# Three crossbar transposes a unit on the SP queue, and five exponential buffers for seven, in a fused attention and gated MLP kernel

## The chip, the cores and the metric

The kernel runs on one core of a Trainium2 chip. The metric is the device time of one execution in microseconds; lower is better. A core has five engines that run their own instruction streams in order and meet through semaphores: TensorE (PE, with its weight loads shown apart as PEld), VectorE (DVE), ScalarE (ACT), GpSimd (POOL) and SyncE (SP), which here only issues DMA transfers. The transfers themselves run on 16 DMA engines.

## The reference

Attention over 4 batches and 8 heads, 576 positions, head dimension 64, with a bias that a small MLP of the relative position gives, and behind it a gated MLP on the 2304 x 512 result. All of it is float32.

```
scores = scale * q @ k.T                      # (4, 8, 576, 576)
x      = log1p(|i - j|) / log1p(max(i, 1))
scores = scores + relu(x * w1 + b1) @ w2      # a bias per head, the same for all batches
attn   = softmax(scores)
y      = (attn @ v), heads side by side       # (2304, 512)
out    = (sigmoid(y @ w_gate) * (y @ w_val)) @ w_out
```

## The kernel before, in words

There are three phases. The first builds the bias of all heads (up to about 105 us). The second is the attention, in 16 units of work; a unit is one batch and one pair of heads. The third is the gated MLP. The change lies in the attention.

A unit has nine steps, s = 0 to 8. Steps 0 to 7 each take 128 query rows of one head (four steps per head); step 8 takes the last 64 rows of both heads. Every step n of the 144 runs through one body, written out by hand (the scheduler does not reorder: `tc.manual_schedule`), so the order of the Python calls is the order of instructions on each engine:

- `score(n)`: TensorE multiplies q by k into a PSUM tile `sc` (L569). It hands back `soft`, which is called later in the same step: one VectorE instruction (L573) adds the bias, writes the negated scores to a tile `en` and gives the row minimum `mn`; one ScalarE instruction (L576) takes the exponential in place and sums the row.
- `turn(n - 2)`: two steps later TensorE transposes that `en`, four blocks of 128 x 128 (L592), into a PSUM tile `pt`, of which there are three in a ring. Out of `pt` ScalarE writes the high part `aH` (L491) and VectorE the low part `aL` (L492), each in a format TensorE takes. In steps s = 1, 4, 7 of the set `AR` ScalarE copies `pt` to SBUF (L605) and GpSimd makes both parts.
- The last 64 columns of `en` are not transposed then. In `turn` of s = 3 and s = 7, that is in step 5 and in step 0 of the next unit, four narrow transposes (L612) read the columns 512 to 576 of four `en` tiles at once: those of s - 3, s - 2, s - 1 and s. So an `en` of s = 0 is still read in step 5, and one of s = 4 in step 0 of the next unit.
- `products`: TensorE multiplies the transposed parts by v into `acc` (L654), 36 instructions a unit, `FILL[s]` of them at the end of each step; VectorE copies `acc` out as `xe` (L657) and SP stores it.

The order on VectorE inside a step: in steps of the set `SOFT` (2, 7, 5, 3) `soft` comes first and the low parts of the step before (`after`) follow it; in the other steps they come ahead of `soft`.

SP gets, over a unit: in step 0 the load of k (`kr`), in step 1 that of v (`vr`), in step 2 two small stores of row sums (`rs`), in step 3 the four copies that spread q over the tile `QS` of the next unit and the load of q (`qr`), and two stores of `xe`. Each transfer on SP is issued when its own semaphore waits are met, in order; one that waits holds up those behind it. From step 2 of unit 12 on, `extra(n)` also gives the MLP's first loads (`xin`, `xrec`, `ww`) to SP, after what the step itself issues, by a list called `PLAN`.

Tiles of SBUF come from pools. A pool `enp` with `ENB` buffers holds the `en` tiles; a new `en` takes the buffer of the one `ENB` steps back, and its first writer (L573) waits until that one's last reader is done.

Of the kernel before, what the change touches and what calls it, by code (L numbers as in the profile page):

```python
# [13 lines left out]
F16 = mybir.dt.float16  # L14
# [9 lines left out]
HF = S // 2  # L24
NCH = S // 64
FILL = (7, 0, 9, 0, 6, 3, 2, 7, 2)
ENB = 7
WM = 6
LAG, WSTEP, V0STEP, V1STEP = 2, 2, 7, 1
KSTEP, QSTEP = (4, 8), 1  # L30
# [48 lines left out]
AR = (1, 4, 7)  # L79
# [357 lines left out]
def attention(tc, att, q, k, v, biases, biasL, ident, xs, rs, extra):  # L437
# [3 lines left out]
    nc = tc.nc  # L441
    PSUM = bass.MemoryType.PSUM
    pool = lambda n, b, **kw: att.enter_context(tc.tile_pool(name=n, bufs=b, reuse_waits="tile", **kw))
# [18 lines left out]
    def load_k(u):  # L462

        p, b = units[u]
        qkraw[u, "kr"] = t = raw.tile([128, 2, S], F32, name="kr")
        for g in range(2):
            nc.sync.dma_start(out=t[64 * g:64 * g + 64], in_=k[b, 2 * p:2 * p + 2].rearrange("h d s -> d h s"))
# [22 lines left out]
    def split(hi, lo, ps):  # L490
        nc.scalar.activation(out=hi, in_=ps, func=AF.Copy)  # L491
        return lambda: nc.vector.tensor_tensor(out=lo, in0=ps, in1=hi.bitcast(F32), op=ALU.subtract)  # L492

    def pool_split(hi, lo, src):
        copy(hi, src)
        nc.gpsimd.tensor_tensor(out=lo, in0=src, in1=hi.bitcast(F32), op=ALU.subtract)  # L496

    def prep_k(u, h):
        if h == 0:
            prepped[u] = two.tile([128, 2, 2, S], F32R, name="k"), QS[u % 2]  # L500
        pool_split(prepped[u][0][:, h, 0], prepped[u][0][:, h, 1], qkraw[u, "kr"][:, h])
# [26 lines left out]
    vp = pool("vp", 1)  # L528
    enp = pool("enp", ENB)
    st = pool("st", 4)  # L530
# [2 lines left out]
    at4 = pool("at4", 2)  # L533
    ar_p = pool("arp", 2)
    xep = pool("xep", 2)
    ps_t = pool("ps_t", 3, space=PSUM)
    ps_v = pool("ps_v", 1, space=PSUM)
    ps_s = pool("ps_s", 2, space=PSUM)
# [5 lines left out]
        vsplit[u, h] = vv  # L544

    state = {}

    def score(n):
        u, s = divmod(n, 9)
        p, b = units[u]  # L550
        ks, qs = prepped[u]
        if s == 0:
            state[u] = (st.tile([128, 9], F32, name="sm"), [], [], at4.tile([128, 2, S], F32R, name="a4"), {})
        ps = ps_s.tile([128, 2, 512], F32, name="sc")
        en = enp.tile([128, S], F32, name="en")
        sm = state[u][0][:, s:s + 1]
        state[u][4][s] = en
        if s < 8:
            h, it = divmod(s, 4)
            nbias = biases[0][:, 8 * p + s] if p < 3 else biases[1][:, s]  # L560
            i = slice(128 * it, 128 * it + 128)
            w = qs[:, (S + 128) * h:(S + 128) * h + 512][:, i]
            mms = [(w, ks[:, h, 0]), (w, ks[:, h, 1])]
        else:
            nbias = biasL[:, p]
            mms = [(qs[:, 512 + 64 * h:640 + 64 * h], ks[:, h, r]) for r in range(2) for h in range(2)]
        for i, (l, r) in enumerate(mms):
            for e in range(2):
                nc.tensor.matmul(out=ps[:, e, 0:HF], lhsT=l, rhs=r[:, HF * e:HF * e + HF], start=(i == 0), stop=(i == len(mms) - 1))  # L569
        mn = st.tile([128, 1], F32, name="mn")  # L570

        def soft():
            nc.vector.tensor_tensor_reduce(  # L573
                out=half(en), in0=ps[:, :, 0:HF], in1=half(nbias), scale=-0.125, scalar=3.0e38,
                op0=ALU.add, op1=ALU.min, accum_out=mn)
            nc.scalar.activation(out=en, in_=en, func=AF.Exp, bias=mn, scale=-1.0, accum_out=sm)  # L576

        return soft

    def turn(n):  # L580

        u, s = divmod(n, 9)
        p, b = units[u]
        sm, aH, aL, a4, ens = state[u]
        en = ens[s]
        after = []
        if s in (0, 4):
            aH.append(atp.tile([128, 4, S], F32R, name="aH"))
            aL.append(atp.tile([128, 4, S], F32R, name="aL"))
        pt = ps_t.tile([128, 4, 128], F32, name="pt")  # L590
        for J in range(4):
            nc.tensor.transpose(pt[:, J], en[:, 128 * J:128 * J + 128], ident)  # L592
        if s == 8:
            for h in range(2):
                after.append(split(aH[h][:, :, 512:576], aL[h][:, :, 512:576], pt[:, :, 64 * h:64 * h + 64]))
            pt = ps_t.tile([128, 4, 128], F32, name="pt")
            nc.tensor.transpose(pt[0:64, 0], en[:, 512:576], ident)
            last = normal(u, pt)
            after.append(split(a4[0:64, :, 512:576], a4[64:128, :, 512:576], pt[0:64, 0].rearrange("p (h i) -> p h i", h=2)))
            return after + [last]  # L600
        h, it = divmod(s, 4)
        i = slice(128 * it, 128 * it + 128)
        if s in AR:
            ar = ar_p.tile([128, 4, 128], F32, name="ar")
            nc.scalar.activation(out=ar, in_=pt, func=AF.Copy)  # L605
            pool_split(aH[h][:, :, i], aL[h][:, :, i], ar)
        else:
            after.append(split(aH[h][:, :, i], aL[h][:, :, i], pt))
        if it == 3:
            pt = ps_t.tile([128, 4, 128], F32, name="pt")  # L610
            for e in range(4):
                nc.tensor.transpose(pt[0:64, e], ens[s - 3 + e][:, 512:576], ident)  # L612
            after.append(split(a4[0:64, h, 0:512], a4[64:128, h, 0:512], pt[0:64].rearrange("p e i -> p (e i)")))
        return after

    def normal(u, pt):
        p, b = units[u]
        nc.tensor.transpose(pt[0:9, 2], state[u][0], ident)
        rt = rtp.tile([9, 128], F32, name="rt")

        def leave():
            nc.vector.tensor_copy(out=rt, in_=pt[0:9, 2])
            to = rs[2 * p:2 * p + 2, S * b:S * b + S]
            nc.sync.dma_start(out=to[:, 0:512].rearrange("h (i p) -> h i p", p=128), in_=rt[0:8])
            nc.sync.dma_start(out=to[:, 512:576].rearrange("(o h) p -> o h p", o=1), in_=rt[8:9].rearrange("o (h p) -> o h p", h=2))

        return leave

    def invert(u):
        sm = state[u][0]  # L630
        nc.scalar.activation(out=sm, in_=sm, func=AF.Identity, bias=tiny)
        return lambda: nc.vector.reciprocal(out=sm, in_=sm)
# [31 lines left out]
    NU = len(units)  # L664
    with tc.manual_schedule():
        work = iter(())
        after, due, loads, slow = [], [], [], []
        for n in range(9 * NU + LAG + 1):
            u, s = divmod(n, 9)
            soft = score(n) if n < 9 * NU else None  # L670
            inverse = invert(u - 1) if s == 0 and u > 0 else None
            later = turn(n - LAG) if LAG <= n < 9 * NU + LAG else []
            if s in KSTEP and u + 1 < NU:
                prep_k(u + 1, KSTEP.index(s))
                if s == KSTEP[1] and u + 2 < NU:
                    loads.append(lambda z=u + 2: load_k(z))
            if s == QSTEP and u + 1 < NU:
                o, lower = prep_q(u + 1)
                later.append(lower)
                slow = [lambda o=o, z=u + 1: spread_q(z, o)]  # L680
                slow += [lambda z=u + 2: load_q(z)] if u + 2 < NU else []
            elif slow:
                loads, slow = loads + slow, []
            if soft and s in SOFT:
                soft()
                soft = None
            for f in after:
                f()
            for f in due:
                f()  # L690
            due, loads = loads, []
            if soft:
                soft()
            after = later
            if inverse:
                inverse()
            if s == WSTEP and 0 < u < NU:
                work = products(u - 1)
            if n == 9 * NU + LAG - 1:
                work = products(u - 1)  # L700
            for _ in range(FILL[s] if n < 9 * NU else 9):
                f = next(work, None)
                if f:
                    after.insert(0, f)
            if s == V0STEP and u < NU:
                split_v(u, 0)
            if s == V1STEP and 0 < u < NU:
                split_v(u - 1, 1)
                load_v(u)
            if n == 9 * NU:  # L710
                split_v(u - 1, 1)
            extra(n)
        for f in after:
            f()
        for f in work:
            if f:
                f()
# [562 lines left out]
```

## Time and profile before

| | us |
|---|---|
| median of 3 runs | 791.5 |
| lowest and highest | 790.57, 792.73 |
| span of the profiled execution, first to last instruction | 789.5 |
| TensorE busy | 755.9 (96%) |
| VectorE busy | 650.9 (82%) |
| ScalarE busy | 573.4 (73%) |
| GpSimd busy | 371.9 (47%) |
| DMA moved | 114.00 MB |

The profiled execution's own time is its span of 789.5 us and what a launch puts around it; the median of the runs is 2.0 us above that span. The busy times are sums over three unlike phases, so they do not say what limits the attention; the rows below are from that phase.

### The profile page before, as it was taken

Reading aid. Unit: us, or ns where it says so; the run is one execution under the profiler, and the core shown is the slowest. Engines: PE = TensorE matmul, PEld = TensorE weight load, DVE = VectorE, ACT = ScalarE, POOL = GpSimd, SP = SyncE. Lnnn points to the kernel's source line nnn. Section 1 sums busy time; section 2 is a strip of 40 time slices with the busy share of each in tenths; the row PEclk is TensorE's granted clock in tenths of the full one; section 3 lists DMA queues with packets and bytes.
Section 4 is the critical chain, followed back from the end, with each engine's and each line's share of the span. In section 5 each row is a group of like instructions: output and inputs, shape, how many; then the busy total and the mean of one; then the engine's idle time right before and its main releaser. Section 6 shows DMA issues by size and latency. Waiting matters only on the chain.

```text
span 789.5 us, 17579 instructions
## 1 busy us (share of the span) xinstructions
PE 755.9 (96%) x6358; PEld 605.0 (77%) x6358; DVE 650.9 (82%) x1329; ACT 573.4 (73%) x1222; POOL 371.9 (47%) x433
## 2 busy tenths in 40 slices
PE   7999989999999999898999999998999999999997
PEld 4888879999999998897899999964555555555553
DVE  6788888998999999997598988869998886777762
ACT  5888859989998998776676666676666667666653
POOL 2233559999999997972010120047633331534100
PEclk9999999999999999999999999999999999999999
DMA  6544444664665568735898953347612212422102
GB/s 201 157 147 128 122 109 109 182 171 137 165 173 152 146 171 220 205 122 182 302 288 240 271 151 119 124 125 195 180 56 80 81 54 76 154 65 81 54 2 80
DMA packets 66775, 114.00 MB, mean 144 GB/s; under 512 B 7808, under 2 KB 29440, under 8 KB 66688
## 3 DMA queue, kind: packets, MB, share of 16 engines
q1 hardware_dynamic: 62208, 106.78, 44.5%
q0 software_dynamic: 2560, 3.15, 2.6%
q10 hardware_dynamic: 1920, 2.95, 1.1%
q8 instruction: 50, 0.82, 0.4%
q14 instruction: 37, 0.30, 0.1%
HBM read 79.75 MB, written 23.67 MB: 131 GB/s over the span
## 4 chain that ended last, share of the span: by engine, by line
PE 73%; DVE 13%; ACT 5%; issue 3%; DMA 2%; SPq 1%; POOL 1%; ACTq 0%; DVEq 0%
PE po L928 15%; PE pg L1081 10%; PE sc L569 8%; PE acc L654 8%; PE pu L1081 7%; PE pt L592 6%; PE pu L904 6%; PE pg L904 6%; PE bps L362 3%; DVE btmp L370 2%; PE y L338 2%; ACT ind L343 1%; PE pt L612 1%; DVE bias L378 1%; DVE wv L1050 1%
## 5 line engine op out<-in xcount | busy, mean ns | idle before, releaser
L1081 PEld LDWEIGHTS <-wv 128*128 128x128 f16 x1008 | 98.1, 98 | 84.9 <-issue 9.9
L576 ACT ACTIVATE en<-en,mn 128x576 f32<-128x576 f32 x144 | 111.6, 775 | 31.1 <-DVE mn L573 29.9
L1039 POOL TENSOR_TENSOR ws<-wm 128x256 f32<-128x256 f32 x44 | 41.4, 942 | 157.6 <-DMA wm<-scratch 100.6
L569 PE MATMUL sc<-k,QS 128*128 128x288 f32 x640 | 112.1, 301 | 2.1 <-DMA QS<-part 0.8
L1081 PE MATMUL pg<-xq,wv 128*128 128x384 f16 x576 | 109.3, 326 | 3.1 <-ACT c L1107 2.3
L573 DVE CUSTOM_DVE_ANT_0 en<-sc,bias 128x576 f32<-128x576 f32 x128 | 93.8, 751 | 7.3 <-PE sc L569 6.3
L569 PEld LDWEIGHTS sc<-k,QS 128*128 128x128 f32 x640 | 92.1, 189 | 3.4 <-issue 1.0
L592 PE MATMUL pt<-ident,en 128*128 128x128 f32 x576 | 87.4, 274 | 3.6 <-DVE aL L492 2.0
L928 PE MATMUL po<-wo,gh 128*128 128x512 f16 x288 | 85.7, 379 | 0.0
L1081 PE MATMUL pu<-xq,wv 128*128 128x384 f16 x432 | 82.0, 326 | 2.2 <-DVE c L1087 2.2
L654 PE MATMUL acc<-aH,vv 128*128 128x288 f32 x240 | 76.2, 334 | 2.7 <-DVE xe L657 2.7
L980 POOL DMA_DIRECT2D xt<-xs x32 | 26.9, 1076 | 108.3 <-DMA xt<-xs 94.9
L1087 DVE TENSOR_TENSOR c<-pu,c 128x384 f32<-128x384 f32 x72 | 39.9, 555 | 41.6 <-PE pu L1081 28.1
L592 PEld LDWEIGHTS pt<-ident,en 128*128 128x128 f32 x576 | 69.0, 141 | 6.8 <-ACT en L576 2.9
L492 DVE TENSOR_TENSOR aL<-pt,aH 128x512 fp32r<-128x512 f32 (+1 forms) x112 | 66.6, 607 | 7.1 <-ACT aH L491 7.1
L362 PE MATMUL bps<-cfs,ind 128*128 128x64 bf16 x1458 | 67.4, 193 | 2.9 <-DVE bias L378 2.4
L343 ACT ACTIVATE ind<-y 128x576 bf16<-128x576 f32 x100 | 62.2, 653 | 10.0 <-PE y L338 7.7
L654 PE MATMUL acc<-aL,vv 128*128 128x288 f32 x240 | 66.9, 296 | 0.0
L362 PEld LDWEIGHTS <-ind 128*128 128x128 bf16 x1458 | 58.6, 98 | 9.2 <-DVE bias L378 4.2
L1099 ACT ACTIVATE gh<-c 128x384 f16<-128x384 f32 x48 | 25.1, 523 | 55.5 <-DVE c L1097 54.0
L496 POOL TENSOR_TENSOR aL<-ar,aH 128x512 fp32r<-128x512 f32 x48 | 62.5, 1302 | 3.9
L491 ACT ACTIVATE aH<-pt 128x512 fp32r<-128x512 f32 (+1 forms) x112 | 57.6, 529 | 1.2 <-PE pt L592 1.2
(173 smaller groups left out, 1948.2 us busy)
## 6 DMA issues: line engine op xcount, KB each, us to landing
wm<-scratch SPq DMA_DIRECT2D x48, 256.0 KB
kr<-in_k_dram SPq DMA_DIRECT2D x32, 288.0 KB
QS<-part SPq DMA_DIRECT2D x64, 144.0 KB
xs<-xe SPq DMA_DIRECT2D x32, 288.0 KB
scratch<-wm SPq DMA_DIRECT2D x27, 256.0 KB
wo<-scratch SPq DMA_DIRECT2D x24, 256.0 KB
vr<-in_v_dram SPq DMA_DIRECT2D x16, 320.0 KB
qr<-in_q_dram SPq DMA_DIRECT2D x16, 288.0 KB
```

Of the source, the lines that this page charges most:

```text
L343: nc.scalar.activation(out=o, in_=y[:, :, 0:HF], func=AF.Sigmoid, scale=float(2.0 ** 64))
L362: nc.tensor.matmul(out=o, lhsT=st, rhs=cfs[:, part], start=(part == 0), stop=(part == 2))
L492: return lambda: nc.vector.tensor_tensor(out=lo, in0=ps, in1=hi.bitcast(F32), op=ALU.subtract)
L496: nc.gpsimd.tensor_tensor(out=lo, in0=src, in1=hi.bitcast(F32), op=ALU.subtract)
L569: nc.tensor.matmul(out=ps[:, e, 0:HF], lhsT=l, rhs=r[:, HF * e:HF * e + HF], start=(i == 0), stop=(i == len(mms) - 1))
L573: nc.vector.tensor_tensor_reduce(out=half(en), in0=ps[:, :, 0:HF], in1=half(nbias), scale=-0.125, scalar=3.0e38, op0=ALU.add, op1=ALU.min, ...
L576: nc.scalar.activation(out=en, in_=en, func=AF.Exp, bias=mn, scale=-1.0, accum_out=sm)
L592: nc.tensor.transpose(pt[:, J], en[:, 128 * J:128 * J + 128], ident)
L654: nc.tensor.matmul(out=acc[:, 0:HF], lhsT=l, rhs=r, start=(i == 0), stop=(i == len(mms) - 1))
L904: self.nc.tensor.matmul(out=(pg, pu)[z], lhsT=l, rhs=r, start=(kc == 0 and i == 0), stop=(kc == 3 and i == 2))
L928: self.nc.tensor.matmul(out=po, lhsT=l[:, tt], rhs=r, start=(first and i == 0), stop=(last and i == 2))
L1081: nc.tensor.matmul(out=p, lhsT=W[i][:, l, at + kc], rhs=V[b][:, r, kc], start=(new and n == 0), stop=(n == 5), skip_group_check=not new)
```

## The change

`ENB` goes from 7 to 5. A new pool `xbar` holds a tile `flat` of 128 x 1024 16-bit zeros, which GpSimd clears once, and one buffer named `crossed`. In steps s = 1, 4 and 7 of every unit SP gets a DMA that transposes `flat` into a new `crossed`: 128 x 1024 becomes 128 x (8 x 128), 256 KB read from SBUF and 256 KB written to it, 48 times in all. Nothing reads `crossed`. As the pool has one buffer, each of these transfers waits on SP until the one before has landed. The call stands behind `score` and `invert` and ahead of `turn`, so in a step the transpose stands on SP ahead of the step's other transfers.

```
-ENB = 7
+ENB = 5
...
+    xbar = pool("xbar", 1)
...
+    flat = xbar.tile([128, 1024], F16, name="flat")
+    nc.gpsimd.memset(flat, 0.0)
+
+    def cross(s):
+        if s in AR:
+            t = xbar.tile([128, 8, 128], F16, name="crossed")
+            nc.sync.dma_start_transpose(out=t, in_=flat)
...
             inverse = invert(u - 1) if s == 0 and u > 0 else None
+            if n < 9 * NU:
+                cross(s)
             later = turn(n - LAG) if LAG <= n < 9 * NU + LAG else []
```

## Rows read from the trace of the kernel before

**Rows 1.** Busy time by stretch: three stretches of 25 us inside the attention.

```profile
core 0: us, PE busy (x) PEld busy (x) DVE busy (x) ACT busy (x) POOL busy (x), PEclk, DMA share, GB/s
205.00:230.00 25.00, 25.00 (x203) 24.91 (x203) 22.75 (x55) 22.22 (x55) 22.89 (x25) 1.00 0.53 144
280.00:305.00 25.00, 25.00 (x204) 24.91 (x202) 22.75 (x55) 22.23 (x55) 19.66 (x23) 1.00 0.76 192
305.00:330.00 25.00, 22.32 (x173) 21.15 (x172) 23.23 (x54) 21.18 (x51) 24.17 (x25) 1.00 0.68 191
```

**Rows 2.** Chain that ended last: start, us, what.

```profile
317.98 2.45 DMA QS<-part
```

**Rows 3.** What VectorE waited for, 130 to 296 us: total, times, longest.

```profile
DVE en L573 <- PE sc L569: 4.5, 11, 0.4
```

**Rows 4.** Timeline of VectorE: start, us, what, in brackets idle before and releaser.

```profile
128.03 0.76 DVE L573 CUSTOM_DVE_ANT_0 en<-sc,bias 128x576 f32<-128x576 f32 x1 [0.40 <-PE sc L569]
...
219.04 0.76 DVE L573 CUSTOM_DVE_ANT_0 en<-sc,bias 128x576 f32<-128x576 f32 x1 [0.40 <-PE sc L569]
...
219.73 0.69 DVE L492 TENSOR_TENSOR aL<-pt,aH 128x512 fp32r<-128x512 f32 x1
...
294.91 0.76 DVE L573 CUSTOM_DVE_ANT_0 en<-sc,bias 128x576 f32<-128x576 f32 x1 [0.41 <-PE sc L569]
```

**Rows 5.** Timeline of TensorE and its weight loads, steps 5 and 6, same unit.

```profile
218.32 0.69 PE L569 MATMUL sc<-k,QS 128*128 128x288 f32 x4
218.84 0.60 PE L592 MATMUL pt<-ident,en 128*128 128x128 f32 x4
219.28 0.60 PE L612 MATMUL pt<-ident,en 128*64 128x128 f32 x4
...
220.11 0.70 PE L569 MATMUL sc<-k,QS 128*128 128x288 f32 x4
...
220.53 0.49 PEld L592 LDWEIGHTS pt<-ident,en 128*128 128x128 f32 x4
```

**Rows 6.** Instructions on tile `en`, the narrow transposes: ns min/median/max of one.

```profile
L612 PE MATMUL pt<-ident,en x128: 272/273/273, 113.4 to 357.1; 128*64 128x128 f32 x128
```

**Rows 7.** Timeline of VectorE and TensorE, step 0 of the next unit.

```profile
226.26 0.75 DVE L573 CUSTOM_DVE_ANT_0 en<-sc,bias 128x576 f32<-128x576 f32 x1
...
225.96 0.60 PE L612 MATMUL pt<-ident,en 128*64 128x128 f32 x4
```

**Rows 8.** DMA queues (packets, MB, share) and one issue (KB, us to landing).

```profile
q1 hardware_dynamic: 62208, 106.78, 44.5%
...
xt<-xs POOLq DMA_DIRECT2D x32, 96.0 KB, 4.1
```

**Rows 9.** Timeline of SP's queue over one unit: start, us of issuing, transfer.

```profile
221.26 0.38 SPq L660 DMA_DIRECT2D xs<-xe  x1
227.63 1.46 SPq L467 DMA_DIRECT2D kr<-in_k_dram  x2
...
231.04 0.34 SPq L478 DMA_DIRECT2D vr<-in_v_dram  x1
231.52 0.68 SPq L624 DMA_DIRECT2D rs<-rt  x1
...
232.98 2.45 SPq L513 DMA_DIRECT2D QS<-part  x4
```

**Rows 10.** Timeline of TensorE, step 0 that uses that `QS`.

```profile
240.18 0.69 PE L569 MATMUL sc<-k,QS 128*128 128x288 f32 x4
```

**Rows 11.** Timeline of SP's queue and of GpSimd in unit 12.

```profile
295.64 2.52 SPq L513 DMA_DIRECT2D QS<-part  x4
...
298.84 1.27 SPq L807 DMA_DIRECT2D xin<-xs  x2
...
304.65 1.02 POOL L823 TENSOR_TENSOR xin<-xin 128x384 f32<-128x384 f32 x1 [3.33 <-DMA xin<-xs]
```

**Rows 12.** Timeline of TensorE in unit 13.

```profile
312.77 0.63 PE L592 MATMUL pt<-ident,en 128*128 128x128 f32 x4 [0.82 <-DVE aL L492]
```

**Rows 13.** GpSimd: ahead of the attention, and one clearing of a tile.

```profile
109.72 1.42 POOL L506 TENSOR_TENSOR part<-qr,part 128x576 fp32r<-128x576 f32 x1 [3.91 <-issue]
...
L1183 POOL MEMSET ones<- x1: 205/205/205, 359.4 to 359.4; 128x128 bf16 x1
```

## The prediction

> **What bounds the kernel now.** I read the busy time by stretch first. In the middle of the attention TensorE is busy for the whole of 25 us, with the clock granted in full (its level of 2.4 GHz), and VectorE, ScalarE and GpSimd for about 90% of it [rows 1]. Nothing in that stretch makes TensorE wait, so TensorE sets the pace and what delays it there is paid in full. From about 297 us on, in units 12 to 15, it is busy for 22.3 of 25 us [rows 1], and the chain that ended last runs through SP's queue and its transfers [rows 2].
>
> Next I read the waits of VectorE. The largest that repeats is the one I need: L573 waits for the scores, once a unit, 11 times of 0.4 us [rows 3]. The timeline shows it at 128.03 and, eleven units later, at 294.91: a unit takes (294.91 - 128.03) / 11 = 15.17 us, and all eleven look the same [rows 4]. It is step 5, where `soft` comes first on VectorE. VectorE is ahead of TensorE there and starts as soon as the scores are done (218.32 + 0.69 = 219.01; start 219.04).
>
> **Part 1, five buffers.** With seven, no writer of `en` waits for a reader. With five, the `en` of step 5 takes the buffer of step 0, whose last reader is the first of the four narrow transposes of step 5, and the `en` of the next unit's step 0 takes that of step 4, read by the first narrow transpose of that step. The other steps take buffers that these same transposes or earlier ones have left.
>
> Step 5: the narrow transposes begin at 219.28 [rows 5] and one takes 0.27 us [rows 6], so the first is done at 219.55. VectorE follows TensorE by 0.03 us (219.01 to 219.04, above), so L573 starts at 219.58 where it started at 219.04: 0.54 us late. If the wait is for all four, they end at 219.88 and it is 0.87 us late. I take the first, since only that one reads this buffer.
>
> What is late next: behind L573 on VectorE stands the low part of step 2's `pt` (219.73 + 0.69, done at 220.42) [rows 4]. The transposes of step 6 take that same `pt` out of the ring of three, and their weight load starts at 220.53, right behind the scores of step 6 [rows 5]. So only 220.53 - 220.42 = 0.11 us lie between the two, of which some 0.03 to 0.05 go to the semaphore: the slack is 0.06 to 0.08. TensorE then stands still for 0.54 - 0.06 = 0.48, say 0.5 us (0.8 if the wait is for all four). It can't make it up, since it has no idle time, and everything behind moves along with it, so the same wait returns in each unit.
>
> Step 0: the first narrow transpose ends at 225.96 + 0.27 = 226.23, with 0.03 on top 226.26. That is where L573 starts anyway [rows 7]. Nothing is lost.
>
> Units 1 to 12 show this picture: 12 x 0.5 = 6.0 us. In unit 0 TensorE isn't full, and in 13 to 15 VectorE is often the late one (TensorE waits for it, 0.82 us in one place) [rows 12]; for these four I take half, 4 x 0.25 = 1.0, with 0 and 4 x 0.5 as bounds.
>
> **Part 2, the transposes.** The trace has no such transfer. For its share of the DMA engines I take the main queue's rate: 106.78 MB in 44.5% of 789.5 us [rows 8], that is 304 GB/s, so 256 KB fill all engines for 0.86 us. Three a unit are 2.6 us of 15.17, 17 points on a share of 0.53 [rows 1]: it fits. From the end of issuing to landing, a copy of 144 KB within SBUF took 2.45 us [rows 2]; 256 KB lie between that and 256/144 of it, 4.4 us. The worst row is a 96 KB transfer that took 4.1 us [rows 8], in proportion 10.9. Issuing took 0.34 us for `vr` and 0.68 for `rs` [rows 9]; I take 0.6. So 3 to 5 us from issue to landing, call it T, and I take 4.
>
> What hides it: steps 4 and 7 put their transposes behind `qr`, at about 221.2, just ahead of the `xs` store. SP then has nothing to do until `kr` at 227.63 [rows 9]; the second waits there for the first. That of step 1 comes behind `kr` at 229.1, and `vr` is not due before 231.04 [rows 9]. Behind it stand `vr`, `rs` and `QS`. The last of the four `QS` is issued by 235.43 [rows 9], lands some 2.45 us later [rows 2] at 237.9, and TensorE needs it at 240.05, ahead of 240.18 [rows 10]: 2.2 us to spare. So in units 1 to 11 the transposes cost nothing. If that cover goes, each microsecond of lateness beyond 2.2 is one of TensorE.
>
> Unit 12 has no such gap. SP issues `QS`, `qr` and the MLP's loads without a break, and GpSimd waits 3.33 us for `xin` [rows 11], behind which VectorE and then TensorE wait. The transpose of step 4 stands ahead of that `xin`: 0.6 for issuing and 0.86 on the rings, 1.5 us. Bounds are 0, if `xin` was held up by something else, and 5 us, if T comes on top here.
>
> The clearing of `flat` on GpSimd: 128 columns of 16 bits took 0.205 us, so 1024 take 1.6 at most (0.2 at least); GpSimd has 3.91 us idle ahead of 109.72 [rows 13]. Nothing.
>
> **Sum.** 6.0 + 1.0 + 1.5 = 8.5 us on the span of 789.5, so 798.0. The median of the runs is 2.0 above that span: 800.0. The low end of this case is 12 x 0.45 = 5.4 and nothing else, 797; the high end 16 x 0.8 + 5 = 18, 809.5.
>
> **Rivals.**
>
> *The transposes bind.* `crossed` has one buffer, so the three of a unit run one after the other, each with its full T. They fit while 3T is under 15.17 us, T up to about 5.1. By the worst row, T = 10.9, a unit takes 32.7 us, 17.5 more; over 15 units 263 us, about 1055. For it: nothing shows this kind of transfer. Against it: every transfer within SBUF that the chain shows lands in less than half of that [rows 2]. The Trainium skill (VectorE: DVE Perf Modes, The three transpose paths) gives 1309 ns for a crossbar transpose of 128 x 128; if the eight blocks of one of these came one after the other, an estimate by that page is 10.5 us, a unit of 31.4 and 1035 in the end. The same skill (DMA: Bandwidth & Descriptors, Latency and other measured facts) has 261 GB/s for transposes, by which one is 1.0 us of transfer and none of this happens; no run here shows either yet. Chance 0.08.
>
> *The engines crowd in units 12 to 15.* The share there is 0.76 already [rows 1]; with 17 points it is 0.93, and each of these four units would lose 2 to 5 us on `xin`, `xrec` and `QS` instead of the one 1.5: 8.5 - 1.5 + 14 = 21 us, about 812 (806 to 820). Chance 0.10.
>
> *Not slower.* The loss of part 1 is swallowed in units 13 to 15, where TensorE waits anyway. That works if its waits there are for transfers whose time doesn't move with the attention; they have to swallow 6 us of the 2.7 us that it is idle in 305 to 330 [rows 1] and of as much behind. Then 790 to 794. Against it: the loads there are issued in order behind stores of the same units, so they come later too. Chance 0.12. A gain could only come from these same stretches, by a shift that happens to shorten their waits: 786 to 789, chance 0.04.
>
> **How the numbers follow.** The forecast has 0.66, the binding transposes 0.08, the crowding 0.10, no change 0.12, a gain 0.04. A difference of 0.3%, 2.4 us, is about what a measurement of this kernel can tell from none, so faster 0.04, same 0.12, slower 0.84. The range takes the forecast's own, 797 to 809.5, the better half of the no-change case below it and the crowding up to 815: 792 to 815. It leaves out the binding transposes, the gain, the rest of the crowding and some of the no-change case, under 2 in 10 together.
>
> **What would show it.** In the profile after: the wait of L573 in step 5 grows from 0.40 to about 0.95 us and names `pt` L612; TensorE waits for L492 ahead of L592 some 0.5 us once a unit; a unit takes 15.7 us; SP's transposes are issued at once and the engines' share is about 0.7; the scores wait for no `QS`. Wrong would be: a unit above 16 us with waits for `QS` or `kr` (the transposes bind), or one of 15.17 with no new wait (then the buffers are handed out otherwise than I think).

## The result and the profile after

| | before | after |
|---|---|---|
| median of 5 runs, us | 791.5 (790.57 to 792.76) | 799.11 (796.05 to 799.75) |
| ratio, with its 95% interval | | 1.009 [1.0068, 1.0113] |
| span of the profiled execution, us | 789.5 | 797.3 |

The kernel is 0.9% slower, 7.6 us by the medians and 7.8 us by the two profiled spans. The forecast was a span of 798.0 and a median of 800.0. In the changed file everything behind the edit stands eight lines lower: L573 is now L581 (`soft`), L569 is L577 (the scores), L592 is L600 and L612 is L620 (the wide and the narrow transposes). The crossbar transpose is L554.

I read the stretches first, as in the kernel before; [rows 1] answer to these:

```profile
core 0: us, PE busy (x) PEld busy (x) DVE busy (x) ACT busy (x) POOL busy (x), PEclk, DMA share, GB/s
205.00:230.00 25.00, 24.41 (x194) 23.66 (x192) 21.51 (x53) 21.27 (x51) 21.61 (x24) 1.00 0.87 223
280.00:305.00 25.00, 24.41 (x193) 23.66 (x193) 21.80 (x55) 22.75 (x56) 22.41 (x25) 1.00 0.84 210
305.00:330.00 25.00, 22.47 (x171) 21.05 (x170) 22.39 (x50) 19.29 (x47) 19.79 (x21) 1.00 1.03 241
```

TensorE, which was busy for the whole of 25 us in the first two stretches [rows 1], now stands still for 0.59 of them. In the first, the three engines behind it each do about 1 us less. The granted clock is still 1.00, its level of 2.4 GHz, so the clock isn't it. The share of the DMA engines has gone from 0.53 to 0.87. These two changes are the two halves of the edit, and a reader who stops here could blame either. The waits tell them apart. VectorE's, 130 to 300 us (total, times, longest):

```profile
DVE en L581 <- PE pt L620: 10.5, 11, 1.0
```

It answers to [rows 3]: the wait of the minimum in step 5 names the narrow transposes in place of the scores, and it has grown from 0.40 to 0.95 us. TensorE has a single line of waits from 130 to 300 us, where the kernel before has none at all from 130 to 296:

```profile
PE pt L600 <- DVE aL L492: 3.3, 11, 0.3
```

The line counts what the matmuls wait, 0.3 us a unit; their weight load, shown below, waits 0.50.

The timeline of VectorE shows the period, for [rows 4]:

```profile
129.64 0.76 DVE L581 CUSTOM_DVE_ANT_0 en<-sc,bias 128x576 f32<-128x576 f32 x1 [0.95 <-PE pt L620]
...
224.28 0.76 DVE L581 CUSTOM_DVE_ANT_0 en<-sc,bias 128x576 f32<-128x576 f32 x1 [0.96 <-PE pt L620]
...
224.96 0.69 DVE L492 TENSOR_TENSOR aL<-pt,aH 128x512 fp32r<-128x512 f32 x1
...
303.13 0.76 DVE L581 CUSTOM_DVE_ANT_0 en<-sc,bias 128x576 f32<-128x576 f32 x1 [0.95 <-PE pt L620]
```

A unit takes (303.13 - 129.64) / 11 = 15.77 us where it took 15.17: 0.60 more. TensorE and its weight loads in the same step, for [rows 5]:

```profile
223.00 0.69 PE L577 MATMUL sc<-k,QS 128*128 128x288 f32 x4
...
223.97 0.60 PE L620 MATMUL pt<-ident,en 128*64 128x128 f32 x4
...
224.80 0.70 PE L577 MATMUL sc<-k,QS 128*128 128x288 f32 x4
...
225.76 0.42 PEld L600 LDWEIGHTS pt<-ident,en 128*128 128x128 f32 x4 [0.50 <-ACT a L491]
```

The scores end at 223.69, but L581 starts at 224.28, which is 0.04 behind the end of the first narrow transpose (223.97 + 0.27). The low part L492 behind it ends at 225.65, and the weight load of the transposes that need its ring place starts at 225.76. Before, that load came 0.42 us after the start of step 6's scores (220.11 to 220.53) [rows 5]; now it comes 0.96 after (224.80 to 225.76). That is 0.54 of the 0.60. The releaser printed there, ScalarE's L491, is only the one that came last by the records; the line of waits above has the right name.

SP's queue over one unit, for [rows 9], and then what its transposes waited for from 130 to 300 us, which is the one buffer:

```profile
218.81 1.27 SPq L554 DMA_TRANSPOSE crossed<-flat  x1
...
222.90 2.47 SPq L513 DMA_DIRECT2D QS<-part  x4
...
226.05 1.29 SPq L554 DMA_TRANSPOSE crossed<-flat  x1
227.44 0.52 SPq L668 DMA_DIRECT2D xs<-xe  x1
229.69 1.24 SPq L554 DMA_TRANSPOSE crossed<-flat  x1
232.78 1.66 SPq L467 DMA_DIRECT2D kr<-in_k_dram  x2
```

```profile
SPq L554 <- DMA crossed<-flat: 19.0, 12, 1.9
```

Issuing a transpose takes SP 1.27 us, twice what I took, but there is still idle time behind two of the three (1.73 and 1.85 us). Behind that of step 1 SP goes on without a break until the `xs` store ends at 227.96. The page's queue and packet lines, for [rows 8]:

```profile
DMA packets 117462, 126.58 MB, mean 159 GB/s; under 512 B 58496, under 2 KB 80128, under 8 KB 117376
...
q1 hardware_dynamic: 112896, 119.37, 53.4%
```

The queue had 62208 packets and 44.5% [rows 8]. So a transpose is (112896 - 62208) / 48 = 1056 packets, all of them under 512 bytes (58496 in place of 7808 in the whole program), and fills all 16 engines, by the queue's share, for (0.534 x 797.3 - 0.445 x 789.5) / 48 = 1.55 us.

### The profile page after: what moved, and what is told of

Same layout as the page of the kernel before. It is cut to its first block, busy times and chain, and to the rows that moved or that the text cites. A ratio compares the mean times of both kernels' runs of the same rounds, so it can differ in the third digit from the quotient of the medians.

```text
span 797.3 us, 17637 instructions
## 1 busy us (share of the span) xinstructions
PE 759.8 (95%) x6358; PEld 605.2 (76%) x6358; DVE 651.8 (82%) x1329; ACT 573.4 (72%) x1222; POOL 373.3 (47%) x434
## 2 busy tenths in 40 slices
DMA packets 117462, 126.58 MB, mean 159 GB/s; under 512 B 58496, under 2 KB 80128, under 8 KB 117376
## 3 DMA queue, kind: packets, MB, share of 16 engines
q1 hardware_dynamic: 112896, 119.37, 53.4%
## 4 chain that ended last, share of the span: by engine, by line
PE 72%; DVE 15%; ACT 4%; DMA 4%; issue 3%; POOL 1%; SPq 1%; ACTq 0%; DVEq 0%; POOLq 0%
PE po L938 16%; PE pg L1091 10%; PE pu L1091 8%; PE sc L577 7%; PE acc L662 7%; PE pt L600 6%; PE pu L914 6%; PE pg L914 6%; PE bps L362 3%; DVE en L581 2%; DVE btmp L370 2%; DVE aL L492 2%; PE y L338 2%; DVE bias L378 1%; ACT ind L343 1%
## 5 line engine op out<-in xcount | busy, mean ns | idle before, releaser
L1049 POOL TENSOR_TENSOR ws<-wm 128x256 f32<-128x256 f32 x44 | 43.4, 987 | 155.5 <-DMA wm<-scratch 137.8
L577 PE MATMUL sc<-k,QS 128*128 128x288 f32 x640 | 112.7, 303 | 2.2 <-DVE bias L378 0.6
L581 DVE CUSTOM_DVE_ANT_0 en<-sc,bias 128x576 f32<-128x576 f32 x128 | 93.6, 750 | 15.1 <-PE pt L620 13.4
L577 PEld LDWEIGHTS sc<-k,QS 128*128 128x128 f32 x640 | 92.7, 190 | 3.6 <-PE sc L577 0.8
L600 PE MATMUL pt<-ident,en 128*128 128x128 f32 x576 | 88.0, 275 | 7.3 <-DVE aL L492 6.1
L600 PEld LDWEIGHTS pt<-ident,en 128*128 128x128 f32 x576 | 67.4, 141 | 13.8 <-ACT a L491 7.5
L492 DVE TENSOR_TENSOR aL<-pt,aH 128x512 fp32r<-128x512 f32 (+1 forms) x112 | 66.5, 606 | 7.6 <-POOL vv L485 6.0
L491 ACT ACTIVATE aH<-pt 128x512 fp32r<-128x512 f32 (+1 forms) x112 | 57.3, 527 | 1.3 <-PE pt L600 1.3
```

The source lines that it names most:

```text
L581: nc.vector.tensor_tensor_reduce(out=half(en), in0=ps[:, :, 0:HF], in1=half(nbias), scale=-0.125, scalar=3.0e38, op0=ALU.add, op1=ALU.min, ...
```

## The experiments

### Which half costs it

Four kernels: the five buffers alone; the transposes with six buffers; both, with the order of step 5 changed; and both, with the narrow transposes moved ahead.

The buffers alone (kernel before):

```
-ENB = 7
+ENB = 5
```

> Five exponential buffers, no transposes. Theory A (the buffers cost it): L573 of step 5 waits 0.95 us for the narrow transposes, a unit takes 15.65 to 15.77 us and the time is 797.5 to 799. Theory B (the transposes cost it, by their traffic or by SP's queue): a unit takes 15.17 us and the time is 791.5. If the time lies in between, the difference to 799.1 is what the transposes cost.

797.67 us, ratio 1.0079 [1.0066, 1.0092], a unit of 15.77. Its waits of VectorE and of TensorE, 130 to 300 us:

```profile
DVE en L573 <- PE pt L612: 9.6, 10, 1.0
```

```profile
PE pt L592 <- DVE aL L492: 3.3, 11, 0.3
```

The same wait, the same period, with no transpose in the program. The buffers cost nearly all of the loss. What the transposes add here, 1.0090 against 1.0079, is inside the two intervals.

Six buffers and the transposes (changed kernel; the transposes read the bias tile instead of zeros):

```
-ENB = 5
+ENB = 6
...
+    flat = biasL[:, 0, 0:512].bitcast(mybir.dt.uint16)
```

> Six exponential buffers with the three transposes a unit. To make room the transposes read a part of the bias tile of the last rows (as 16-bit numbers) and no tile of zeros; the sizes are the same. Theory A: no writer waits for the narrow transposes, a unit takes 15.17 us and the time is 791.5 to 793.5, what lies above 791.5 being unit 12 and the start. Theory B: a unit takes 15.6 us or more and the time is 797 to 799. Both can't be near 799.

793.68 us, 1.0031 [1.0016, 1.0045]. VectorE's wait is back to what it was before:

```profile
DVE en L580 <- PE sc L576: 4.5, 11, 0.4
```

TensorE has no wait at all between 130 and 300 us, and a unit takes 15.23. With six buffers the `en` of step 5 takes that of step 8 of the unit before, which no narrow transpose of this step reads. The 2.3 us that are left don't come from the middle units, which add 11 x 0.06; the third group looks for them.

The order of step 5 (changed kernel): the low part of the step before now goes ahead of the minimum.

```
-SOFT = (2, 7, 5, 3)
+SOFT = (2, 7, 3)
```

> The changed kernel, but in step 5 the low part of step 2 goes ahead of the bias-and-minimum instruction on VectorE (5 leaves the set SOFT). Theory A (it is the low part, held up behind the waiting instruction, that stops TensorE): the transposes of step 6 find their buffer free, a unit takes 15.2 to 15.4 us and the time is 792 to 795. Rival: the late minimum itself holds up the exponential and so TensorE two steps later; then a unit stays at 15.7 and the time at 798 to 800.

791.74 us, 1.0009 [0.9995, 1.0023], a unit of 15.22, and again no wait of TensorE from 130 to 300 us. VectorE's:

```profile
DVE en L581 <- PE pt L620: 3.3, 12, 0.3
```

The minimum still waits for the narrow transposes, but what TensorE needs no longer stands behind the instruction that waits for it. So the price of five buffers is the in-order wait, not the reuse.

The narrow transposes first (changed kernel): in step 5 and step 0 TensorE does the four narrow transposes ahead of the four wide ones.

```
+        if s in (3, 7):
+            tail = ps_t.tile([128, 4, 128], F32, name="pt")
+            for e in range(4):
+                nc.tensor.transpose(tail[0:64, e], ens[s - 3 + e][:, 512:576], ident)
...
-            pt = ps_t.tile([128, 4, 128], F32, name="pt")
-            for e in range(4):
-                nc.tensor.transpose(pt[0:64, e], ens[s - 3 + e][:, 512:576], ident)
```

> The changed kernel, but TensorE does the four narrow transposes ahead of the four wide ones of the same step. The first narrow one is then done 0.44 us earlier, some 0.1 us after the scores. Theory A: L573 of step 5 starts 0.1 us late and not 0.54, inside or just beyond the slack, a unit takes 15.2 to 15.3 us and the time is 792 to 794.5. Rival (traffic of the transposes): a unit stays at 15.7 and the time at 799.

794.39 us, 1.0039 [1.0024, 1.0053], a unit of 15.34. VectorE's wait, where L601 is now the line of the narrow transposes:

```profile
DVE en L581 <- PE pt L601: 5.7, 11, 0.5
```

The wait shrinks from 0.95 to 0.5 us, because the reader comes earlier by the length of the wide ones. Moving the reader works as moving the waiter does, but it isn't free: 0.12 us a unit stay against the kernel with the other order.

### How near the transposes were to binding

Three kernels on the one above with `SOFT = (2, 7, 3)`, all with five transposes a unit (s = 0, 2, 4, 6, 8) and the bias tile as their source: one buffer; two; and two with 128 x 512.

```
-        if s in AR:
+        if s in (0, 2, 4, 6, 8):
```

> e3_minimum_later with five transposes a unit (steps 0, 2, 4, 6, 8) in place of three, read from the bias tile as in e2_six_and_cross, still one buffer for what they write. In the changed kernel the next transpose goes out about 3.5 us after the start of the one before where SP has nothing else, 1.27 of it for issuing. Theory C (the chain of single transposes binds as soon as they no longer fit into a unit): 5 x 3.5 = 17.5 us against 15.2, so a unit of 17 to 18.5 us, waits for QS or k on TensorE, 820 to 840 us. Rival (the DMA engines or SP's issuing have room and the waits overlap with SP's other work): a unit of 15.3 to 15.6 us, 793 to 798 us.

878.02 us, 1.1109 [1.1082, 1.1136]: slower by 87 us, so the direction was right and the size two to three times too low. SP's timeline in one unit, in which `x2` is two transposes, the second of which waits for the first:

```profile
201.99 4.28 SPq L553 DMA_TRANSPOSE crossed<-biasL  x2
206.36 1.38 SPq L467 DMA_DIRECT2D kr<-in_k_dram  x2
...
212.78 2.65 SPq L513 DMA_DIRECT2D QS<-part  x4
215.49 0.59 SPq L473 DMA_DIRECT2D qr<-in_q_dram  x1
216.14 6.36 SPq L553 DMA_TRANSPOSE crossed<-biasL  x2
```

and the stretches of 2 us where TensorE runs dry:

```profile
core 0: us, PE busy (x) PEld busy (x) DVE busy (x) ACT busy (x) POOL busy (x), PEclk, DMA share, GB/s
...
212.00:214.00 2.00, 0.84 (x5) 0.37 (x3) 1.85 (x5) 1.01 (x4) 1.92 (x3) 1.00 0.79 164
214.00:216.00 2.00, 0.00 (x0) 0.00 (x0) 0.48 (x1) 1.14 (x3) 1.89 (x3) 1.00 0.93 218
216.00:218.00 2.00, 1.93 (x9) 1.91 (x10) 0.00 (x0) 0.00 (x0) 1.86 (x3) 0.56 0.89 208
218.00:220.00 2.00, 2.00 (x12) 1.89 (x11) 0.89 (x3) 1.61 (x3) 1.92 (x3) 0.59 0.69 153
220.00:222.00 2.00, 2.00 (x18) 1.98 (x18) 1.66 (x3) 1.09 (x6) 1.92 (x3) 1.00 0.00 0
```

Here SP holds the loads back in order. From 130 to 300 us it waits 24 times, 44.1 us in all, for the transpose before, and from 105 to 440 us the scores wait 10 times, 34.7 us in all, for `QS`. In the stretch shown TensorE stands still for 2.9 us, put down to GpSimd, which had itself waited 4.63 us for that late `kr`. When TensorE starts again the granted clock is 0.56 and 0.59, near its lower level of 1.2 GHz, for these two stretches; it does 9 and 12 matmuls where it does 18 at 1.00. So the stop is paid for a second time. Over 25 us the engines' share is between 0.68 and 0.84 from 130 to 330 us, so it isn't their bandwidth.

Two buffers:

```
-    xbar = pool("xbar", 1)
+    xbar = pool("xbar", 2)
```

> e5_five_crossings with two buffers to write to, so that no transpose waits for the one right before it. Theory C: the chain is gone; what is left is traffic, 5 x 1.55 us a unit on the 16 DMA engines (from the growth of the main queue's share) beside a share of 0.53 to 0.67: just full, a unit of 15.3 to 16 us, 793 to 803 us. Rival (it was the traffic that bound, not the one buffer): the same as e5_five_crossings within 3 us.

822.0 us, 1.0371 [1.0349, 1.0393]. The one buffer was 56 of the 87 us. The rest was expected to vanish and didn't. The eight stretches of 25 us from 130 to 330 us have shares of 0.95 to 1.08, and TensorE waits for `QS` (9 times, up to 5.7 us). SP still waits 15.4 us for a buffer from 130 to 300 us, where one buffer made it 44.1. Beside that, two things were left: the engines' share, and SP's time for issuing. Half the bytes tell them apart:

```
-            t = xbar.tile([128, 8, 128], mybir.dt.uint16, name="crossed")
+            t = xbar.tile([128, 4, 128], mybir.dt.uint16, name="crossed")
```

> e6_two_buffers with transposes of 128x512, half the bytes. If issuing on SP goes with the blocks (1.27 us for eight): 0.7 to 0.8 us each, SP has 5 x 0.55 us more room a unit, the traffic halves too, and a unit is back at 15.2 to 15.3 us: 791 to 794 us. If issuing is a fixed cost of a transpose: 1.2 us still; then a unit of 15.2 shows that the traffic bound e6_two_buffers, and one of 16 us or more that SP's queue did.

805.47 us, 1.0185 [1.0158, 1.0212]. Its issues (ns min/median/max) and one stretch:

```profile
L553 SPq DMA_TRANSPOSE crossed<-biasL x80: 1189/1262/2412, 55.6 to 371.4; - x80
```

```profile
280.00:305.00 25.00, 24.13 (x194) 23.79 (x193) 21.79 (x54) 21.61 (x51) 19.97 (x22) 1.00 0.80 193
```

Half the size takes off half of what was left (from 31 to 14.7 us), so the transfer itself was part of it, be it by the engines' share or by the wait for a buffer, which falls from 15.4 to 4.1 us. The other half stays at a share of 0.80, where the changed kernel runs with 0.87 and no wait for it. A transpose of half the size costs SP as much to issue, 1.26 us. By the sum of its issues SP is taken for 0.88 of the time from 150 to 300 us (0.70 in the changed kernel, 0.45 before, over units 1 to 11). I read this as SP's queue falling behind: units 1 to 7 take 15.2 us and only the next four 15.4 to 16.8. The trace bears the lag out: the copies to `QS` begin 0.13 us ahead of step 5's minimum in unit 1, 1.24 behind it in unit 7 and 3.53 behind it in unit 9; with three transposes and the same order they are never more than 0.65 behind up to unit 11. But no run took SP's issuing away and left the transfers, so that the issuing makes the lag is argued and not shown. The lag in units 1 to 11 is also the smaller part: at step 5 of unit 12 the kernel is 5.2 us behind the kernel before, and at that of unit 15 it is 12.4.

### What one transpose costs, and where

Plain copies (the kernel with `SOFT = (2, 7, 3)`, the same 256 KB and the same waits, no crossbar):

```
-            nc.sync.dma_start_transpose(out=t, in_=flat)
+            nc.sync.dma_start(out=t.rearrange("p a b -> p (a b)"), in_=flat)
```

> e3_minimum_later with three plain copies of the tile of zeros in place of the three transposes: the same 256 KB each, the same places on SP's queue, one buffer. If it matters that they are transposes: issuing falls from 1.27 to 0.35 to 0.6 us, the share on the rings from 1.55 to about 0.9 us each, and a unit from 15.22 to 15.17 us. If only the bytes matter, a unit stays at 15.22. Either way 790.5 to 793 us, too close for the clock; the unit and the share tell.

788.66 us, 0.9964 [0.9948, 0.998].

```profile
L554 SPq DMA_DIRECT2D crossed<-flat x48: 475/482/587, 4.5 to 356.1; - x48
```

```profile
q1 hardware_dynamic: 69120, 119.37, 48.5%
```

The copy is 144 packets instead of 1056 and (0.485 x 788.7 - 0.445 x 789.5) / 48 = 0.65 us of the engines instead of 1.55, and its issue takes 0.48 us instead of 1.27. It is faster than the kernel before, which the copies can't be the reason for; the last group shows that about half of that is the order of step 5; the rest is within the intervals.

The transposes in the last four units only (the kernel with six buffers):

```
-            if n < 9 * NU:
+            if 9 * 12 <= n < 9 * NU:
```

> e2_six_and_cross with the transposes in units 12 to 15 only. If the last units pay for them (the step of the prediction that gave unit 12 1.5 us): units 1 to 11 take 15.17 us, units 12 and 13 are 1 us longer each as in e2_six_and_cross, and the time is 792.5 to 794. If what e2_six_and_cross lost are the 0.06 us of each unit: 791.0 to 792.0.

793.7 us, 1.0035 [1.0022, 1.0048], against 1.0031 with all 48. So 36 of the 48 transposes cost nothing that can be measured, and the price lies in the last units. Two lines show one place where it may arise, of ScalarE's timeline and of the chain that ended last:

```profile
363.19 0.63 ACT L867 ACTIVATE w<-ww 128x512 fp32r<-128x512 f32 x1 [3.19 <-DMA crossed<-biasL]
```

```profile
356.77 6.18 DMA crossed<-biasL
```

The last transpose lands 6.18 us after its issue began, and an early tile of the MLP waits for it. Nothing reads `crossed`, yet here something waits for it. From the first gate matmul to the first output matmul this kernel takes 16.58 us, the one with all 48 transposes and six buffers 13.58, and the kernel before and the changed one 12.4. That these tiles wait because they take the place of `crossed` is what the releaser suggests; I didn't move the place to show it. Nor is it the whole price: the three kernels with five transposes a unit have the same wait (8.7, 5.0 and 4.1 us), but the one with all 48 and six buffers lacks it in its trace and has the same median. The list of issues also has the time from issue to landing, which it leaves open elsewhere:

```profile
crossed<-biasL SPq DMA_TRANSPOSE x12, 3.2
```

The trace times only three of these twelve, at 3.0 to 3.5 us; the last one isn't among them.

### The order alone

The kernel before with both of these edits, and with the second alone; neither has a transpose.

```
-ENB = 7
+ENB = 5
...
-SOFT = (2, 7, 5, 3)
+SOFT = (2, 7, 3)
```

> Five exponential buffers, no transposes, and the low part ahead of the minimum in step 5 (e3_minimum_later without its transposes). If the order alone makes five buffers as good as seven: 790.5 to 792. If e7_plain_copies was faster than the kernel before because of this order (unit 0 took 14.72 us with it and 15.16 without): 788 to 790, faster than before by 0.2 to 0.4%.

789.35 us, 0.9983 [0.9969, 0.9996], a unit of 15.22.

> The kernel before, seven buffers, with only the order of step 5 changed. If the gain of e7_plain_copies comes from the order: 788 to 790, units of 15.17 us. If it came from something that five buffers bring (addresses, or which tiles of the MLP lie where): 791 to 792, as before.

789.14 us, 0.998 [0.9968, 0.9993], a unit of 15.17. The order by itself gains 0.2%, with either number of buffers, and both beat the kernel before by a hair. Against the middle units it brings nothing (15.17 as before). From the start of step 6's minimum in unit 12 (297.99 before, 297.42 here) to the last minimum of the attention (356.24, 354.07) it is 1.6 us shorter (58.25 and 56.65 us), so that is where the trace with seven buffers has it. But with five buffers and this order the same way takes 58.39 us (298.10 to 356.49), so where the order gains stays open. With five buffers and this order the 48 transposes cost 1.0009 against 0.9983, some 2 us, and 48 copies nothing (0.9964).

## Why the prediction was right

The forecast came true with its mechanism, and its sum came out at 797.3 for 798.0. That the sum is so close is partly luck: single terms are off by up to 1.1 us and cancel. Since the units 1 to 11 look alike, the sum can be taken apart. The times run from the first minimum of the attention (107.35 before, 107.99 after) over step 5 of units 1, 12 and 13 to the first gate matmul (363.19, 371.66) and the end.

| term | predicted | measured |
|---|---|---|
| units 1 to 12, buffers | 12 x 0.5 = 6.0 | 11 x 0.60 + 0.49 = 7.09 |
| units 0 and 13 to 15, buffers | 1.0 | 0.37 |
| unit 12, transpose ahead of `xin` | 1.5 | 0.36 |
| ahead of the attention | none | 0.64 |
| the MLP | none | -0.63 |
| sum, us of span | 8.5 | 7.83 |

The start of the minimum in step 5 is itself 0.54 late in units 1 to 12, which counts for the unit behind it. So unit 0 lost (129.64 - 107.99) - (128.03 - 107.35) - 0.54 = 0.43, and units 13 to 15 gained 0.06. Unit 12 took 16.36 us from its step 5 to the next, 16.31 with the buffers alone (0.54 - 0.05 = 0.49 lost) and 16.67 in the changed kernel (0.36 more). All of this comes from one execution of each kernel, and only the 0.60 is a mean over units; the five runs of the changed kernel spread over 3.7 us.

**The wait in step 5** was predicted at 0.54 us and for the first of the four narrow transposes, not for all. It is 0.55 longer (0.40 to 0.95), and L581 starts 0.04 behind that first one. Had it been for all four, L581 would have stood until 224.57.

**What is late next** was the low part and, behind it, the weight load of step 6, with a slack of 0.06 us. The load comes 0.54 later, not 0.48. So there was no slack worth the name: that load already started 0.11 behind the low part before, and it does so now (225.65 to 225.76). The 0.06 was too fine a reading of a gap that is simply what the hand-over takes. In the terms of the sum, TensorE's stop of 0.48 was undersized by this and by the 0.05 that follows: a unit lost 0.60.

**The rest of the 0.60** is another 0.05. All kernels without seven buffers have it, also where TensorE waits for nothing: 15.22 or 15.23, with six buffers, with five and the other order, with and without transposes. With seven and the other order it is 15.17. So it comes with the number of buffers. What in it does so stays open.

**The transposes in units 1 to 11** were to cost nothing, and don't: with the other order these units take 15.22 us with three transposes each and 15.22 without any. The time T from issue to landing, 3 to 5 by my reckoning, is 3.2 for the three that are timed; in the middle of the attention the next one goes out 3.64 us after the one before (226.05 to 229.69). That they would be issued at once was wrong as a sign: SP waits up to 1.9 us for the one before, as the working on what hides them had it, and nothing behind them needed that time. Two prices that stood behind this were too low: issuing 1.27 for 0.6, the engines 1.55 for 0.86. They were covered too, since SP idles and the share of 0.53 left room. The share that I named as a sign, about 0.7, was wrong accordingly: it is 0.87.

**Unit 12** was half a mistake. GpSimd's wait for `xin` grew from 3.33 [rows 11] to 3.61 us, where it is 3.36 with the buffers alone:

```profile
313.06 1.02 POOL L833 TENSOR_TENSOR xin<-xin 128x384 f32<-128x384 f32 x1 [3.61 <-DMA xin<-xs]
```

I put the issue and the transfer on the path in full. The transpose's issue there does stand ahead of that `xin` and takes 1.52 us, but by then the buffers had made everything else in the unit late too.

**Step 0** lost nothing, as predicted: the list of waits has L581 behind the narrow transposes once a unit, not twice. The clearing of `flat` took 0.96 us, at 1.4 us into the program: the tile is made ahead of the attention's loop, and nothing waited for it.

**The two terms that I had not** are the start of the attention and the MLP, and they cancel. The first minimum of the attention stands between 106.72 and 107.35 us in the four kernels without any transpose (before, the buffers alone, and the two of the order), and between 107.21 and 108.56 in the three that issue the first one at about 4 us. One of these is earlier than the kernel before, so a part of the 0.64 may be that transfer, or it may be the difference of one execution to another. The five that read the bias tile issue none before 55 us and scatter as widely (106.98 to 108.85), which speaks for the second. That stays open, as do the 0.63 of the MLP.

**The rivals.** That the transposes bind was right as a mechanism and far off in this kernel: with 3T near 10 us there is room, and it took five a unit to bring it about, most of it by the one buffer. My point of decision, T above 5.1, left out that SP has other things to issue and that these wait in line too. The Trainium skill (VectorE: DVE Perf Modes, The three transpose paths) gives 1309 ns for one block of 128 x 128; the estimate of 10.5 us for eight of them in turn is refuted by the 3.2 above: eight blocks in one transfer don't take eight times that. The Trainium skill's 261 GB/s (DMA: Bandwidth & Descriptors, Latency and other measured facts) comes, as an estimate, to 1.0 us of transfer; the traces have 1.55 of the engines' time. *The crowding* was to begin with the engines' share at 0.93 in units 12 to 15; the share is 1.03 there in 305 to 330 us, and no crowding shows in this kernel: from step 5 of unit 13 to that of 15 it takes 38.00 us where it took 38.06. *Not slower* needed the late stretches to swallow the loss; they did so for 0.6 us of the 1.0 that units 0 and 13 to 15 were given and for none of the rest.

## What to carry to other kernels

When a pool gets fewer buffers, find for each writer the last reader of the buffer it now takes, and then look at what stands behind that writer on its own engine: the cost is what another engine needs from there, and putting that ahead of the waiting instruction takes the cost away (797.67 to 789.35 us here, with the same five buffers). A transfer that nothing reads cost nothing in units 1 to 11 here, where its queue and the engines had room, but it still has to be counted three ways: its share of the engines, its time to issue, and what its buffer holds up. An order that was tuned with one number of buffers should be tried again with the next: here it gained 0.2% even at the old number.

## What was not expected of the hardware

- A crossbar transpose of 128 x 1024 16-bit elements takes SP 1.27 us to issue and one of 128 x 512 takes 1.26; a plain copy of the larger size takes 0.48.
- The same transpose is 1056 packets and 1.55 us of all 16 engines, the copy 144 packets and 0.65 us.
- The share of the DMA engines can read 1.03 over 25 us while the way from step 5 of unit 13 to that of unit 15 takes no longer than before (38.00 us for 38.06).
- After 2.9 us without a matmul TensorE's granted clock was 0.56 and 0.59 in the next two stretches of 2 us, and 1.00 in the one behind them.
- The last of the transposes, in the kernel that has them in the last four units, took 6.18 us from the start of its issue to landing, by the chain that ended last, where the three that are timed took 3.0 to 3.5.
